# Lent weight room, one more kept K tile, a mean summed ahead and a new order in a two-layer decode kernel

## The chip, the core and the metric

The kernel runs on one core of a Trainium2 chip, as one launch. The metric is the device time of one execution in microseconds. Three runs of the kernel before gave 302.71, 304.16 and 307.49 us, median 304.16. One more execution was recorded by the profiler; all stretches and durations below come from it.

## What is computed

Four rows of 512 numbers (x) go through attention, a gated unit, the same attention and the same gated unit again; each step adds to x. Attention reads a cache of keys and values: 4 batch rows (b), 8 heads of keys and values, 4096 positions, 128 numbers each, bf16. Four query heads share one cache head. Both layers read the same cache and the same weights.

```python
def _A_ref(x, k_cache, v_cache, wq, wo):
    q = (x @ wq).reshape(B, Sq, Hq, Dh).transpose(0, 2, 1, 3)
    k = jnp.repeat(k_cache, rep, axis=1)
    v = jnp.repeat(v_cache, rep, axis=1)
    scores = jnp.einsum("bhqd,bhkd->bhqk", q, k) * (Dh ** -0.5)
    p = _softmax(scores, axis=-1)
    o = jnp.einsum("bhqk,bhkd->bhqd", p, v)
    return o.transpose(0, 2, 1, 3).reshape(B, Sq, Hq * Dh) @ wo
def _B_ref(x, w_gate, w_up, w_down):
    return (_sigmoid(x @ w_gate) * (x @ w_up)) @ w_down
x = A_x
x = x + _A_ref(_layernorm(x), k_cache, v_cache, wq, wo)
x = x + _B_ref(_layernorm(x), w_gate, w_up, w_down)
x = x + _A_ref(_layernorm(x), k_cache, v_cache, wq, wo)
x = x + _B_ref(_layernorm(x), w_gate, w_up, w_down)
```

## The kernel before

**Units.** Attention is cut into 16 units, each written b hg l: batch row b, head half hg (4 of the 8 cache heads), layer l. `UNITS` fixes their order: 000 010 100 011 110 200 001 111 210 300 211 310 101 201 311 301. A unit has 8 tiles of K and 8 of V: head s = 0 to 3, half of the positions q = 0 or 1, 512 KB each (128 partitions of 4096 bytes).

**Kept tiles.** Units with hg = 1 load their 16 tiles in layer 0 and leave them in place until layer 1 of the same row has used them (`tile` and `fresh`, lines 520 to 528: a tile is not loaded again where l = 1 and hg = 1). So 010 to 011, 110 to 111, 210 to 211 and 310 to 311 each hold 16 places. Units with hg = 0 load their tiles twice.

**The ring.** K and V tiles live in 23 places (`SLOTS`, the tensor `slots`). Weights have their own tensors: wq (two halves of 2 MB), wo (four parts of 1 MB), wg, wu and wd (1.75 MB each).

**The loads.** All loads are issued by SyncE (SP in the profile) in the order of the string `LOADS`, through `load_kv` (L544) and `load_w` (L552). A word is a weight or a piece of a unit: K2002 stands for two separate loads of unit 200, K010b for head 1 of unit 010 with both halves in one load of 1 MB, for which two neighbouring places must be free. SP works in order: if a load must wait for its place, all later loads wait behind it. The DMA engines work off what has been issued.

**A unit's work.** `queries` forms the unit's queries (PE, ACT) and writes them to `qz` (DVE, L739); for l = 1 it needs the finished x of its row. `unit_scores`: DVE transposes each freshly loaded K tile in place (L762), PE multiplies it with the queries into the PSUM bank `S_ps[i % 2]` (L770). `unit_probs`: the maximum, the exponential and a transposition (L792 to L837). `unit_values`: PE multiplies with the V tiles into `O_ps` (L900), ACT copies (L912), PE and DVE bring the result to `oT` (L919, L927); in layer 0 PE multiplies with wo and DVE adds to x (L941, L953). A place is free again when its last reader is done: PE L770 for K, PE L900 for V.

**The chain.** After unit b10, `chain(b)` runs the gated unit of row b in layer 0: `layer_norm` (L963 to L975; it uses `sq` as scratch), `rstd` (L984 to L993, the power on POOL), `gate_up` (L1003), `gated` (L1030 to L1042), `down` (L1055), x (L1078), and `layer_norm` and `rstd` again for the second attention. Units b01 and b11 cannot start their queries before it.

**The end.** The last V tiles to arrive are those of unit 301. `project` multiplies the last heads with wo (L1098, L1109). `last_chain` then forms the mean of x (DVE L1125, PE L1129 with a matrix of -1/512), subtracts it (`centre`, L1117), takes the squares (L1134, L1139, L1144, power L1151), runs the gated unit for all four rows at once (L1003, L1030, L1035, L1042), brings x into row form in three bf16 parts (L1175, copy L1179), multiplies with wd in 56 matmuls of 128 columns (L1185), joins both with one DVE instruction (L1194) and stores the output with four DMAs, two from SP and two from ACT (L1202).

**The planner.** All instructions are put into a plan with a cost, a rank and an optional shift per stage (`SHIFTS`); `_Plan.schedule` lists them per engine ahead of time: the instruction that can start first, and among equals the one of lowest rank. `slot_for` takes, for each load, the place that becomes free first. What it lists is the fixed order of each engine; waits are semaphores. Where PE would be idle it puts matmuls without use (L1228), which keep the clock up.

## Time and profile before

| | us |
|---|---|
| median of three runs | 304.16 |
| the profiled execution, its own time | 303.01 |
| its span, first to last instruction | 301.3 |
| PE busy | 221.0 |
| DVE busy, of it K transpositions (L762) | 168.2, 115.6 |
| ACT busy | 61.1 |
| granted TensorE clock, mean share | 0.977 |

The chain that ended last consists to 54% of the span of DMA transfers into `slots`, to 25% of PE and to 12% of DVE. 114.57 MB are loaded: 28 loads of 1 MB and 136 of 512 KB for K and V, and nine for the weights. In the parts of the page, a busy share is of one engine; DMA is the mean over the 16 DMA engines. A row of stretches gives, for a stretch of the span, its length, each engine's busy time with the count of instructions, the granted clock, the share of DMA and the rate in GB/s. In a row of the timeline stand the start, the duration, the engine, the line, the operation and, in brackets, the idle time of the engine ahead of it and what ended it.

### The profile page before, as it was taken

How to read it: one execution, taken by the hardware profiler on the slowest of the kernel's cores; microseconds unless marked ns; L12 is line 12 of the kernel's file. 1: busy time of each engine (PE TensorE's matmuls, PEld its weight loads, DVE VectorE, ACT ScalarE, POOL GpSimd, SP SyncE). 2: the span in 40 equal slices, each digit the busy share in tenths (PEclk: the TensorE clock that was granted, in tenths of full speed). 3: DMA queues.
4: the chain of work that ended last, by engine and by line, in shares of the span. 5: the costliest groups of instructions: out<-in, count | busy, mean ns of one | idle time of the engine just before them, and what ended most of it. 6: DMA issues, size and time to landing. Idle time of an engine off the chain costs nothing.

```text
span 301.3 us, 8952 instructions
## 1 busy us (share of the span) xinstructions
PE 221.0 (73%) x4010; PEld 134.8 (45%) x4010; DVE 168.2 (56%) x323; ACT 61.1 (20%) x154; POOL 13.0 (4%) x48
## 2 busy tenths in 40 slices
PE   1202504758797769887999798898986888989895
PEld 1201301435365436544566454446645445554463
DVE  4499436204214967795127977116899781287313
ACT  0200200200312210024322111422320233224211
POOL 8200000000000000000000000000000000000000
PEclk9999999998999997999999799999999799999999
DMA  6999999999999999999999999998899999999940
GB/s 256 429 422 413 419 390 424 407 401 412 415 421 381 328 401 411 411 414 407 407 407 406 411 413 413 411 397 333 289 405 413 406 411 408 410 399 406 406 172 3
DMA packets 28086, 115.14 MB, mean 382 GB/s; under 512 B 2832, under 2 KB 2832, under 8 KB 24336
## 3 DMA queue, kind: packets, MB, share of 16 engines
q1 hardware_dynamic: 28000, 114.57, 95.6%
q8 instruction: 31, 0.51, 0.7%
q14 instruction: 7, 0.06, 0.1%
q10 hardware_dynamic: 48, 0.01, 0.0%
HBM read 114.56 MB, written 0.00 MB: 380 GB/s over the span
## 4 chain that ended last, share of the span: by engine, by line
DMA 54%; PE 25%; DVE 12%; SPq 3%; issue 3%; ACT 2%; DVEq 0%; ACTq 0%
DMA slots<-in_A_v_cache_dram 29%; DMA slots<-in_A_k_cache_dram 25%; DVE slots L762 7%; PE O_ps L900 5%; PE S_ps L770 4%; PE PT_ps L1228 3%; SPq L544 3%; PE M_ps L941 2%; PE G_ps L1055 2%; PE M_ps L919 1%; PE Q_ps L690 1%; PE G_ps L1003 1%; PE Q_ps L706 1%; DVE stat L792 1%; SPq L552 1%
## 5 line engine op out<-in xcount | busy, mean ns | idle before, releaser
L762 DVE STREAM_TRANSPOSE slots<-slots 128x1024 int32<-128x1024 int32 x96 | 115.6, 1227 | 25.7 <-DMA slots<-in_A_k_cache_dram 24.3
L770 PE MATMUL S_ps<-slots,qz 128*32 128x512 bf16 x512 | 39.2, 431 | 36.5 <-DVE slots L762 34.7
L1228 PE MATMUL PT_ps<-even 128*128 128x256 bf16 x453 | 64.9, 283 | 1.2 <-ACT pt_sb L827 1.2
L1228 PEld LDWEIGHTS PT_ps<-even 128*128 128x128 bf16 x453 | 40.8, 101 | 18.9 <-issue 11.3
L900 PE MATMUL O_ps<-slots,pt_sb 128*16 128x512 bf16 x496 | 35.9, 383 | 16.0 <-DMA slots<-in_A_v_cache_dram 12.0
L770 PEld LDWEIGHTS S_ps<-slots,qz 128*32 128x32 bf16 x512 | 13.0, 101 | 52.9 <-DVE slots L762 38.2
L912 ACT ACTIVATE b<-O_ps 128x512 bf16<-128x512 f32 x31 | 18.5, 596 | 72.3 <-PE O_ps L900 59.4
L806 ACT ACTIVATE pp<-S_ps,tr 128x512 bf16<-128x512 f32 x16 | 13.3, 831 | 40.6 <-DVE tr L799 21.6
L900 PEld LDWEIGHTS O_ps<-slots,pt_sb 128*16 128x16 bf16 x496 | 9.1, 87 | 27.2 <-issue 14.1
L927 DVE TENSOR_TENSOR oT<-M_ps,rl 128x8 bf16<-128x8 f32 x31 | 4.7, 152 | 29.4 <-PE M_ps L919 29.1
L941 PE MATMUL M_ps<-oT,wo 128*128 128x64 bf16 x512 | 19.7, 195 | 0.9 <-DVE oT L927 0.6
L941 PEld LDWEIGHTS M_ps<-oT,wo 128*128 128x128 bf16 x512 | 17.5, 99 | 6.0 <-DVE oT L927 2.2
L792 DVE TENSOR_REDUCE stat<-S_ps 128x1 f32<-128x512 f32 x16 | 10.9, 681 | 9.4 <-PE S_ps L770 9.2
L919 PE MATMUL M_ps<-sel_o,b 128*64 128x64 bf16 x496 | 14.0, 200 | 2.4 <-ACT b L912 1.5
L919 PEld LDWEIGHTS M_ps<-sel_o,b 128*64 128x64 bf16 x496 | 10.6, 113 | 10.9 <-ACT b L912 6.2
L993 POOL TENSOR_TENSOR stat<-stat 128x1 f32<-128x1 f32 x8 | 4.4, 549 | 251.1 <-ACT stat L989 251.1
L827 ACT ACTIVATE pt_sb<-PT_ps 128x512 bf16<-128x512 f32 x16 | 9.5, 597 | 15.0 <-PE PT_ps L817 15.0
L953 DVE SCALAR_TENSOR_TENSOR x<-M_ps,x 128x4 f32<-128x4 f32 x16 | 2.4, 153 | 14.9 <-PE M_ps L941 14.9
L734 ACT ACTIVATE maskrs<-mask,stat 128x16 f32<-128x16 f32 x16 | 4.4, 301 | 23.3 <-DVE qz L739 22.0
L812 DVE STREAM_TRANSPOSE pp<-pp 128x256 int32<-128x256 int32 x16 | 6.9, 430 | 4.1 <-ACT pp L806 4.0
L1055 PE MATMUL G_ps<-pp,wd 128*128 128x64 bf16 x224 | 7.5, 191 | 2.1 <-issue 1.1
L739 DVE TENSOR_TENSOR qz<-Q_ps,maskrs 128x256 bf16<-128x256 f32 x16 | 6.3, 397 | 4.9 <-PE Q_ps L729 4.0
(133 smaller groups left out, 165.9 us busy)
## 6 DMA issues: line engine op xcount, KB each, us to landing
slots<-in_A_k_cache_dram SPq DMA_DIRECT2D x68, 512.0 KB, 8.2
slots<-in_A_v_cache_dram SPq DMA_DIRECT2D x68, 512.0 KB, 9.8
slots<-in_A_k_cache_dram SPq DMA_DIRECT2D x14, 1024.0 KB, 13.9
slots<-in_A_v_cache_dram SPq DMA_DIRECT2D x14, 1024.0 KB, 14.5
wq<-in_A_wq_dram SPq DMA_DIRECT2D x2, 2048.0 KB, 18.6
wo<-in_A_wo_dram SPq DMA_DIRECT2D x4, 1024.0 KB, 17.8
wg<-in_B_w_gate_dram SPq DMA_DIRECT2D x1, 1792.0 KB, 18.5
wu<-in_B_w_up_dram SPq DMA_DIRECT2D x1, 1792.0 KB, 17.3
```

Of the source, the lines that this page charges most:

```text
L544: return e.dma_start(o, src)
L762: "dve", lambda e, t=t: e.transpose(ring[t.slot].bitcast(dt.int32), ring[t.slot].bitcast(dt.int32)),
L770: fns.append(lambda e, s=s, t=t, nn=nn, q=q: e.matmul(S_ps[qi][32 * s:32 * s + 32, :], lhsT=window(qi, s * NQ + nn, q), rhs=ring[t.slot].r ...
L792: dve(lambda e: e.tensor_reduce(ml[at], bank, AX.X, ALU.max, negate=True), keys(f"S{qi}", ss), keys("ml", ss), 0.7)
L806: lambda e: e.activation(p_sb[at].rearrange("p (t j r) -> p t r j", j=32, r=2), bank.rearrange("p (t r j) -> p t r j", r=2, j=32), ACTF.Ex ...
L827: "act", lambda e: e.activation(pt_sb[qi][:, cols], PT_ps[:, cols], ACTF.Copy),
L900: fns.append(lambda e, m=m, at=at, v=v, c=c, q=q: e.matmul(O_ps[m:m + 16, :], lhsT=pt[:, at:at + 16], rhs=ring[v.slot][:, c * 512:(c + 1) ...
L912: "act", lambda e: e.activation(b1[:], O_ps[:], ACTF.Copy),
L919: fns.append(lambda e, tt=tt, r=r, a=a: e.matmul(M_ps[64 * a:64 * a + 64, r * SP:(r + 1) * SP], lhsT=b1[:, bass.ds(tt * P + r, 64, step=2) ...
L941: fns.append(lambda e, k=k, n=n, h0=h0: e.matmul(M_ps[:, k * MORE:(k + 1) * MORE], lhsT=wo[:, h0 + n, k * P:(k + 1) * P], rhs=oT[:, b, h0 ...
L1055: fns.append(lambda e, k=k, c=c, rows=rows: e.matmul(o_ps[:, k * MORE:(k + 1) * MORE], lhsT=wd[:, c, k * P:(k + 1) * P], rhs=rows.unsqueez ...
L1228: S.filler(lambda e: e.matmul(PT_ps[:, 0:256], lhsT=ident, rhs=flat_even[:, 0:256], start=True, stop=True), "PT")
```

## The change

- The string of the loads is another permutation of the same pieces, with one tile less: `EXTRA` names K tile (b 3, hg 0, s 3, q 1), which stays in the ring from unit 300 to unit 301 and is not loaded a second time. The loads of 1 MB are 40 instead of 28, and 512 KB loads 111 instead of 136. Which heads are loaded whole is now noted per unit and head.
- The planner's places are 23, then 2 for each part of wo, 3 each in wg, wu and wd, and 8 in wq. Places in wo, wg, wu and wd can be given to tiles until the weight's own load, which waits until they are no longer read (`lend`, `closes`). Places in wq can be used once the last instruction that reads that half of wq is done (`inherit`). A tile that is kept between layers (`stays`) is never put there. A 1 MB load needs two neighbours in the same tensor (`run`).
- The mean at the end: DVE sums the rows of wo for heads 8 to 15 (four reductions over 2 x 512 numbers, stage `sums`) and keeps the sums, times -1/512, as two bf16 parts. `mean_so_far` forms the mean of x before the last two projections; `mean_ahead` adds the share of the last eight heads, eight matmuls of four columns for each four heads, into the same PSUM bank. `last_chain` no longer has L1125 and L1129.
- The product with wd at the end has 28 matmuls of 256 columns; even and odd chunks go to separate halves of the partitions, except the last two. Two DVE instructions on 64 partitions x 256 join it (`lower`, then the output), x in row form is 64 x 256, and two DMAs store the output.
- `SHIFTS` has other values for most stages, so the order on every engine is another.

```diff
+EXTRA = "K3031"
-LOADS = "wq0 K100d K000b K000d K000a K010b K100c K000c K010d wq1 K010a V000a wo1 wo0 K1000 K010c V000c V000b V010b V010d wo2 V000d wo3 K1002 V010c wg V010a wu wd V100d V100c K0011 K2002 K2001 K2003 V1001 K2000 K0012 K110b K110a V1000 K1101 K1103 K0010 V110a K0013 V110b V1102 V1103 V2002 V2003 V2000 V2001 V0012 V0013 K3000 K2100 K3002 K3003 K210c K3001 K2102 K210d V0011 V2101 V0010 V2100 V210d V210c V3000 V3002 V3001 V3003 K2011 K3103 K2010 K1010 K3101 K1011 K1013 K3102 K3100 K1012 V3101 V3100 K2012 K2013 V3102 V3103 V1010 V1011 V2012 V2013 V1012 K3011 K3010 V1013 K3012 K3013 V2010 V2011 V3010 V3011 V301C V301D"
+LOADS = "wq0 K000a K000d K000c K000b wq1 K100c V000d wo0 V000a wg V000c wo2 K010d K1002 wo3 K010c K010a V000b K010b K1000 K100d V010a V010b wo1 V010d V010c wu wd V1000 V1001 K0013 K2002 K2003 K2000 K0011 V100c K2001 K110b K1101 K1103 K110a V100d K0010 V110a K0012 V110b V1102 V1103 V0010 V0011 V2002 V2003 V2000 V2001 K3000 K2100 K3001 V0013 K210c K210d V0012 K3003 K2102 V2101 K3002 V2100 V210d V210c V3002 V3000 V3003 V3001 K1012 K2011 K310b K1010 K310a K1011 K3101 K1013 K3103 K201a V310a K201b V310b K2013 V3102 V3103 V1010 V1011 V1012 V1013 K3013 V2012 K3011 V2013 K301b K301a V301b V201a V201b V301a V301C V301D"
...
+    def lend(self, slots, load):
+
+        load.closes = tuple(slots)
+        self.lent |= set(slots)
+
+    def inherit(self, slots, key):
+
+        t = _Tile(key)
+        t.users = [op for op in self.ops if key in op.keys]
+        for s in slots:
+            self.slots[s] = t
...
+            stays = any(t.stays for t in op.tiles)
+            for s, t in enumerate(tenants):
+                if s in closed or (stays and s in self.lent):
+                    until.append(None)
...
-                if None in until[s:s + n]:
+                if None in until[s:s + n] or self.run[s] != self.run[s + n - 1]:
...
+                    keepers = [u for s in op.closes if tenants[s] for u in tenants[s].users]
+                    if any(u.end is None for u in keepers):
+                        continue
+                    at = max([at] + [u.end + LATENCY[u.eng] for u in keepers])
...
+                for s in op.closes:
+                    if tenants[s]:
+                        op.deps |= set(tenants[s].users)
+                closed |= set(op.closes)
...
-    S = _Plan(SLOTS)
+    S = _Plan([SLOTS, 2, 2, 2, 2, 3, 3, 3, 8])
...
+    room(slots[:].rearrange("p a n -> p (a n)"), SLOTS)
+    for i in range(4):
+        room(wo[:, 8 * i:8 * i + 8].rearrange("p h n -> p (h n)"), 2, f"wo{i}")
+    for key, w in (("wg", wg), ("wu", wu), ("wd", wd)):
+        room(w[:].rearrange("p k n -> p (k n)"), 3, key)
+    room(wq[:].rearrange("p a k n -> p (a k n)"), 8, "wq")
+    double, ring = ring, [r[:, 0:TH * DH] for r in ring]
...
-    def fresh(kind, hg, l, s, q):
-        return not (l == 1 and hg == 1 and (s, q) in kept[kind])
+    def fresh(kind, b, hg, l, s, q):
+        return l == 0 or not (hg == 1 or (kind, b, hg, s, q) in extra)
...
-        S.put("sp", lambda e: e.dma_start(o, i), writes=[key], dma=key, size=size, cost=0.5)
+        op = S.put("sp", lambda e: e.dma_start(o, i), writes=[key], dma=key, size=size, cost=0.5)
+        S.lend(lent.get(key, ()), op)
...
+    mean_ps = S_ps[0][:, 0:B]
+
+    def mean_so_far(rank):
+
+        S.stage = "mean0"
         S.put(
             "dve", lambda e: e.tensor_reduce(xsum, x[:], AX.X, ALU.add),
             reads=[f"x{b}" for b in every_b], writes=[f"xsum{b}" for b in every_b], cost=0.2, rank=rank,
         )
         S.put(
-            "pe", lambda e: e.matmul(U_ps[:, 0:B], lhsT=ones, rhs=xsum, start=True, stop=True),
-            reads=["ones"] + [f"xsum{b}" for b in every_b], writes=["U"], cost=0.35, pairs=2, rank=rank,
-        )
+            "pe", lambda e: e.matmul(mean_ps, lhsT=ones, rhs=xsum, start=True, stop=False),
+            reads=["ones"] + [f"xsum{b}" for b in every_b], writes=keys("S0", range(NS)), cost=0.35, pairs=2, rank=rank,
+        )
+
+    def mean_ahead(h0s, rank):
+
+        S.stage = "mean1"
+        for h0 in h0s:
+            fns = []
+            for h in range(h0, h0 + 4):
+                for part in (0, 1):
+                    fns.append(lambda e, h=h, part=part, h0=h0: e.matmul(
+                        mean_ps, lhsT=wsum[:, part, h - 8:h - 7].broadcast_to([P, P]), rhs=oT[:, :, h],
+                        start=False, stop=(h0 == h0s[-1] and h == h0 + 3 and part == 1),
+                    ))
+            S.put(
+                "pe", fns, reads=[f"oT{b}{h0}" for b in every_b] + ["wsum"], writes=keys("S0", range(NS)), cost=0.0, rank=rank,
+            )
...
         for c0, c1 in cuts:
             fns = []
             for c in range(c0, c1):
                 h = pt_h[:, 64 * (c // 2):64 * (c // 2) + 64].rearrange("p (i r) -> p i r", r=2)[:, 0:B, c % 2]
-                for k in range(KD):
-                    fns.append(lambda e, k=k, c=c, h=h: e.matmul(
-                        S_ps[0][32 * k:32 * k + B, 0:P], lhsT=h, rhs=wd[:, c, k * P:(k + 1) * P], start=(c == 0), stop=(c == FB - 1),
+                upper = 64 * (c % 2) if c1 < FB else 0
+                for z in range(2):
+                    fns.append(lambda e, c=c, h=h, z=z, at=upper + 32 * z: e.matmul(
+                        S_ps[0][at:at + B, 0:256], lhsT=h, rhs=wd[:, c, z * 256:(z + 1) * 256], start=(c < 2),
+                        stop=(c == FB - 1 or (at >= 64 and c == cuts[-1][0] - 1)),
                     ))
...
         S.put(
             "dve",
             lambda e: e.scalar_tensor_tensor(
-                out=rows[:], in0=S_ps[0][:, 0:P], scalar=rs_row, in1=xrow, op0=ALU.mult, op1=ALU.add,
+                out=lower, in0=S_ps[0][64:, 0:256], scalar=rs_row[64:], in1=xrow, op0=ALU.mult, op1=ALU.add,
             ),
...
+        S.put(
+            "dve",
+            lambda e: e.scalar_tensor_tensor(
+                out=b1[0:64, 0:256], in0=S_ps[0][0:64, 0:256], scalar=rs_row[0:64], in1=lower, op0=ALU.mult, op1=ALU.add,
+            ),
+            reads=["S0h0", "rs_row"] + keys("pt_sb0", range(NS)), writes=[own("B1", True)], cost=0.4, rank=rank, lock="B1",
+        )
+        for z in range(2):
             S.put(
-                "act" if k % 2 == 0 else "sp",
-                lambda e, k=k: e.dma_start(out.rearrange("b s (k p) -> k (b s) p", p=P)[k], rows[32 * k:32 * k + B, :]),
-                reads=["xin"], writes=[f"out{k}"], dma="out", cost=0.1, rank=rank,
+                "act" if z == 0 else "sp",
+                lambda e, z=z: e.dma_start(out.rearrange("b s (z p) -> z (b s) p", z=2)[z], b1[32 * z:32 * z + B, 0:256]),
+                reads=[own("B1")], writes=[f"out{z}"], dma="out", cost=0.1, rank=rank,
             )
...
+    S.stage = "sums"
+    for n in range(0, 8, 2):
+        S.put(
+            "dve", lambda e, n=n: e.tensor_reduce(row_sums[:, n:n + 2], wo[:, 8 + n:10 + n, :], AX.X, ALU.add),
+            reads=["wo1"] + ["sq"] * (n > 0), writes=["sq"] if n == 0 else [f"sums{n}"], cost=1.1, rank=rank_v((3, 0, 1), 0),
+        )
+    S.put(
+        "act", lambda e: e.activation(wsum[:, 0], row_sums, ACTF.Copy, scale=-1.0 / D),
+        reads=["sq", "sums2", "sums4", "sums6"], writes=["wsum"], cost=0.2, rank=rank_v((3, 0, 1), 0),
+    )
+    S.put(
+        "dve",
+        lambda e: e.scalar_tensor_tensor(out=wsum[:, 1], in0=row_sums, scalar=-1.0 / D, in1=wsum[:, 0], op0=ALU.mult, op1=ALU.subtract),
+        reads=["sq"], writes=["wsum"], cost=0.17, rank=rank_v((3, 0, 1), 0),
+    )
...
+    mean_so_far(rank_v((3, 0, 1), 0) + 1.0)
     project(8, range(4), rank_v((3, 0, 1), 1) + 1.0, "U")
+    mean_ahead(sorted((8, 12), key=lambda h: place["v", (3, 0, 1), h // 4, 1]), rank_v((3, 0, 1), 1) + 0.5)
     project(8, range(4, 8), rank_v((3, 0, 1), 1) + 1.0, "G")
     last_chain(rank_v((3, 0, 1), 1) + 2.0)
...
+    for i in range(2):
+        S.inherit(lent["wq"][4 * i:4 * i + 4], f"wq{i}")
```

More of the change, by code (lines that the diff above doesn't have):

```diff
@@ L78, in __init__ @@
         self.readers = {}
[L79 removed]
+        self.run = [r for r, n in enumerate(runs) for _ in range(n)]
+        self.slots = [None] * len(self.run)
+        self.lent = set()
         self.stage = ""
```

90 lines of the change are left out of this document (49 added, 41 removed).

## The prediction

> **What bounds the kernel now.** I read the page's slices first, then a table of stretches, then the waits and the timeline of SP, then the timeline of the end.
>
> ```profile
> DMA  6999999999999999999999999998899999999940
> GB/s 256 429 422 413 419 390 424 407 401 412 415 421 381 328 401 411 411 414 407 407 407 406 411 413 413 411 397 333 289 405 413 406 411 408 410 399 406 406 172 3
> HBM read 114.56 MB, written 0.00 MB: 380 GB/s over the span
> ```
>
> The DMA engines are busy nearly all the time; no other engine is above 73%. The rate sags twice, at slices 13 and 14 and at 28 and 29, and there is a tail without transfers. Stretches put numbers to it (last two columns: DMA share, GB/s):
>
> ```profile
> 4.00:94.00 90.00, 44.88 (x748) 28.31 (x748) 39.51 (x67) 10.69 (x25) 5.47 (x25) 0.98 1.02 414
> 94.00:108.00 14.00, 11.62 (x224) 6.65 (x225) 11.94 (x18) 4.26 (x13) 0.55 (x1) 1.00 0.97 341
> 108.00:200.00 92.00, 79.03 (x1362) 48.86 (x1360) 54.56 (x104) 19.96 (x46) 1.10 (x2) 0.96 1.02 411
> 200.00:220.00 20.00, 18.23 (x395) 11.88 (x394) 13.02 (x24) 6.21 (x20) 1.10 (x2) 1.00 0.89 330
> 220.00:286.00 66.00, 55.71 (x1018) 31.89 (x1010) 42.81 (x81) 17.17 (x41) 1.10 (x2) 0.97 1.03 408
> ```
>
> Against 411 GB/s the first sag costs (411 - 341) / 411 x 14 = 2.4 us, the second 81 / 411 x 20 = 3.9 us. Outside them the stream is full. Why the sags come is seen at SP:
>
> ```profile
> SPq L544 <- PE O_ps L900: 77.3, 18, 15.9
> ...
> 95.16 1.83 SPq L544 DMA_DIRECT2D slots<-in_A_k_cache_dram  x2
> ...
> 199.46 0.33 SPq L544 DMA_DIRECT2D slots<-in_A_v_cache_dram  x1
> 199.83 4.31 SPq L544 DMA_DIRECT2D slots<-in_A_k_cache_dram  x3
> ```
>
> SP waits for a place until PE has read a V tile, once for 15.9 us. At 95.16 SP has issued 38.5 MB (counted along `LOADS`), and by the rates above some 38 MB have landed: nothing is queued. The second stop ends at 199.46, when the queue is again short. Both times 16 places hold a kept unit (010, then 210) and seven rotate. They come free when 011 and 211 have run, that is after chain(0) and chain(2): 211's queries are ready at 211.59 (L739) and its scores run 212.07 to 214.09 (L770).
>
> The end:
>
> ```profile
> 292.42 0.64 PE L1098 MATMUL G_ps<-oT,wo 128*128 128x64 bf16 x16
> 293.17 0.17 DVE L1109 TENSOR_TENSOR x<-G_ps,x 128x16 f32<-128x16 f32 x1 [0.80 <-PE G_ps L1098]
> ...
> 293.60 0.39 PE L1129 MATMUL U_ps<-stat 128*128 128x4 f32 x2
> ...
> 294.03 0.17 DVE L1117 TENSOR_TENSOR maskrs<-x,U_ps 128x16 f32<-128x16 f32 x1 [0.48 <-PE U_ps L1129]
> ...
> 298.71 0.35 DVE L1194 SCALAR_TENSOR_TENSOR rows<-S_ps,stat,pt_sb 128x128 bf16<-128x128 f32 x1 [0.70 <-issue]
> 299.09 0.66 SPq L1202 DMA_DIRECT2D out_dram<-rows  x2
> 299.10 0.80 ACTq L1202 DMA_DIRECT2D out_dram<-rows  x2
> ```
>
> From the last V matmul (291.16) to the end of the span lie 10.1 us, one step behind the other.
>
> **The change, part by part.** The sum goes against the profiled 303.01 us (span 301.3 and 1.7 around it); the median is 1.15 higher, two of the three runs lie within 1.2 of it.
>
> *One K tile less:* 0.524 MB / 411 GB/s = 1.28 us, since the stream is the bound. Its transposition goes too (L762, 1.23 us), off the path.
>
> *Twelve more loads of 1 MB in place of 24 halves, 12.58 MB:* the stretch 12 to 20 us, all whole loads, ran at 422 GB/s, 140 to 160, all halves, at 407. That makes 30.9 - 29.8 = 1.1 us at most; the stretch 108 to 200, which mixes them, shows 411, so the bound below is 0. I take 0.6, about the middle. The Trainium skill, "DMA: Bandwidth & Descriptors", section "Rules for kernel authors", asks for at least 1 MiB per DMA for full bandwidth; by that page's 435 GB/s ceiling the term would be an estimated 2.0 us, and the measured 422 says less.
>
> *Room in wo, wg, wu and wd:* nothing gained by itself. It exists only until wd is issued (68.4 before), and 4 to 94 us already runs at 414. Both orders have the same 40 tiles and all weights ahead of V100, 34.9 MB, so wd lands and chain(0) goes on at the same time (before, ACT waits for wd until 89.60). The new wait stands at SP, with every later load behind it. Its cover is the queue: wd was issued 21 us before its use.
>
> *Room in wq:* free only after the queries of 311 and 301 (the last near 271). 220 to 286 runs at 408, so it gains nothing; it pays back the kept tile's place at the end.
>
> *First sag, 2.4 us:* behind wd came V100d and V100c, heads 3 and 2 whole, so the first values could start only when both had landed, and places came free at 95.1. Now V1000 comes first, half 0 of heads 0 and 1: usable 1.05 MB, 2.5 us, sooner, and two places return then. Seven places of K still fill up before 011's scores (98.65), so part stays. Bounds 0 and 2.4; I take 1.2.
>
> *Second sag, 3.9 us:* the count. V210c ends at 76.8 MB, near 192.5 us; K210's places return near 214 and bring data 2 us later: 24 us x 0.411 = 9.7 MB, 18.4 tiles, should go out meanwhile. V300's eight are used and released; some 10.4 K tiles are stuck, with seven places: 3.4 tiles x 1.28 = 4.4 us, near the 3.9 seen. The kept tile, loaded at 70.5 MB, takes one of the seven: +1.28. Against that, chain(2) has slack: the power L993 ran at 210.66 because L984 stood behind the query matmuls, V300's second half was there near 203 but read at 206.0 behind L1055 (1.84 us). With those better placed 211 comes 0.4 to 2 us sooner; bounds of the whole term -2.0 and +2.6 (two tiles), I take +0.3.
>
> *Sums:* four DVE reductions of 1024 numbers, 1.2 us each by L762's 1.23 for as many elements, 5 us with the two small ones. wo1 lands near 73 us; from 75 to 94 DVE works about 5 us. Nothing, by that idle time; without it up to 1.2 us ahead of one transposition, or ahead of chain(0), whose ACT square needs `sq`.
>
> *The end.* L1125 and L1129 with their gaps fill 293.34 to 294.03: -0.69. The last eight matmuls of `mean_ahead` stand ahead of L1098 or just behind it: 16 of L1098 take 0.52 to load, so eight about 0.26: net -0.43. The wd product streams as many columns per strip as before, with half the instructions: 0. The second of the two joining DVE instructions has 256 columns instead of 128; L1035 with 192 took 0.33, with 448 0.62, so 0.41 against 0.35, and `lower` may still run when the last matmuls end: +0.1. One output DMA per queue instead of two: ACT issued for 0.80, so -0.4. Together -0.73; bounds -1.1 and -0.2.
>
> Sum: 303.01 - 1.28 - 0.6 - 1.2 + 0.3 - 0.73 = **299.5 us**.
>
> **The rivals.**
>
> *A, the forecast:* 299.5, own range 297.0 to 301.5. Chance 0.40.
>
> *B, both sags mostly go:* the new order of the chain steps frees 211's places and V300's sooner. 303.0 - 1.3 - 1.1 - 0.7 - 2.4 - 2.0 = 295.5 (294.5 to 298.0). For it: the late reads at 206 and 210.66. Against: the count, by which a shift of 2 us returns at most 1.6 tiles while one place is gone. Chance 0.37.
>
> *C, the kept tile costs a place and no order helps:* second sag +1.28, first unchanged, whole loads 0: 303.0 - 1.28 - 0.7 + 1.28 = 302.3. Chance 0.07.
>
> *D, slower, pairs that aren't free:* K310b and K310a, 1 MB each, stand fourth to sixth in the order behind V300, in the second sag, and need two neighbouring places; unit 310 is kept, so weight rooms are closed to them. Before, all loads there were halves. If no pair is free until 211 has released K210 (214), SP stands from the fourth tile on: three more tiles are late, 3.8 us, plus 1.28 for the place, and with a shorter queue the stretch behind it runs like 200 to 220. 303.0 - 2.6 + 3.8 + 1.3 = 305.5, and more where K201 and V310, also whole, repeat it. It decides if the pair comes later than 203.3, when K2011's second tile went out. Chance 0.13, of it 0.06 above 310.
>
> *E, a weight dams the queue:* a weight's load waits for tiles in its room. From rows: the queue covers about 6.8 MB / 0.411 = 16 us behind wd's issue at 68.4; if the last K100 tile there is read after 84, each microsecond costs one, and chain(0) with it. Before, K1002 was transposed from 71.31. Five too late: 304.5. In the Trainium skill, same page, the section on the anatomy of one DMA has it that DMA engines never wait on semaphores; the issuing sequencer does. The 15.9 us stop of SP agrees. Chance 0.03, of it 0.01 above 310.
>
> **How the numbers follow.** About 2% is what a measurement of this kernel can tell from no change: 298.1 and 310.2 around the median. Faster: B's 0.37 and 0.06 of A, 0.43. Slower: 0.07 from D and E. Within: 0.50. The range 294.6 to 304.8 takes in A, C, E and nearly all of B, and leaves out most of D.
>
> **What would show it.** Bytes 114.04 MB. The stretch 94 to 108 above 341 GB/s, near 375. A sag between 195 and 220 that is still there, about 4 us; if it is gone, B; if SP stops ahead of K310b, D. The first 90 us at 414 or a little more. From the last V matmul to the end of the span 9.4 us instead of 10.1, with no reduction and no matrix of -1/512 between L1098's successor and the centring. I am wrong if the DMA stream is no longer what ends last before the tail.

## The result and the profile after

The changed kernel takes 302.26 us, the median of 20 runs (300.39 to 304.69), against 304.01 us of 20 runs of the kernel before beside it: ratio 0.9937, 95% interval 0.9916 to 0.9959. It is 0.6% faster, which is no change by the bound of 2%. The forecast of 299.5 us lies 4.5 us below the 304.01; 1.75 came. A ratio and its interval leave out runs more than 1.5% above the fastest of their kernel, so that it can differ from the quotient of the medians, which are over all runs.

The profiled execution of the changed kernel took 303.67 us (span 301.9), 1.4 above its own median; that of the kernel before was 1.0 below its. So the two profiles are compared stretch by stretch, and a reading counts where other runs with the same order repeat it. In the changed kernel's lines the loads of K and V are L590 (before L544), transpositions L811, scores L819, V matmuls L949, queries L739 (before L690), `qz` L788, the last projection L1147. The page of the changed kernel, DMA busy tenths and rate by slices, and the bytes:

```profile
DMA  7999999999999999999999999999799999999920
GB/s 255 426 412 407 413 408 405 422 421 407 412 413 408 405 417 415 415 412 403 399 396 361 395 414 416 406 345 358 277 404 418 417 409 388 395 385 416 417 94 1
HBM read 114.04 MB, written 0.00 MB: 378 GB/s over the span
```

The first sag (slices 13 and 14) is gone. There is a new one at slice 22 (361), the one at 27 to 29 is deeper (345, 358, 277), and 34 to 36 are below 400. The same five stretches as before, DMA share and GB/s last:

```profile
4.00:94.00 90.00, 47.46 (x759) 29.94 (x760) 43.00 (x72) 11.11 (x26) 5.46 (x25) 0.81 1.02 413
94.00:108.00 14.00, 12.32 (x240) 7.87 (x241) 12.36 (x17) 4.16 (x13) 0.55 (x1) 1.00 1.03 409
108.00:200.00 92.00, 78.32 (x1343) 47.38 (x1345) 54.63 (x105) 20.32 (x49) 1.10 (x2) 0.94 1.02 402
200.00:220.00 20.00, 17.87 (x365) 11.22 (x365) 12.60 (x24) 6.22 (x18) 1.10 (x2) 0.91 0.85 320
220.00:286.00 66.00, 54.29 (x1024) 31.62 (x1020) 41.44 (x77) 16.69 (x41) 1.10 (x2) 1.00 1.01 406
```

A finer cut, each rate also as time lost against 411 GB/s, (411 - rate) / 411 x length; the last column is the range over three variants with the same loads and another end (below):

| stretch | before | after | the three variants |
|---|---|---|---|
| 94 to 108 | 341, 2.4 us | 409, 0.1 us | 396 to 402 |
| 140 to 170 | 408, 0.2 us | 389, 1.6 us | 383 to 387 |
| 195 to 220 | 345, 4.0 us | 331, 4.9 us | 332 to 341 |
| 245 to 270 | 408, 0.2 us | 394, 1.0 us | 394 to 400 |

So 2.3 us of the first sag are won, and 1.4 + 0.9 + 0.8 us are lost in three later stretches. (They are readings of one profiled execution; the last column shows how far they repeat.) The largest new loss leads to PE, in the second chain. Changed kernel, timeline of PE (start, duration, line, count, idle time before):

```profile
155.62 0.97 PE L739 MATMUL Q_ps<-small,wq 128*128 128x32 bf16 x32
156.43 0.36 PE L1033 MATMUL U_ps<-stat 128*128 128x1 f32 x2
156.66 0.55 PE L739 MATMUL Q_ps<-small,wq 128*128 128x32 bf16 x16
157.14 0.61 PE L949 MATMUL O_ps<-slots,pt_sb 128*16 128x512 bf16 x8
157.68 0.32 PE L739 MATMUL Q_ps<-small,wq 128*128 128x32 bf16 x6
159.07 0.40 PE L739 MATMUL Q_ps<-small,wq 128*128 128x32 bf16 x10 [1.08 <-issue]
...
160.96 3.56 PE L819 MATMUL S_ps<-slots,qz 128*32 128x512 bf16 x32 [0.24 <-DVE qz L788]
```

The same place in the kernel before:

```profile
156.62 0.96 PE L690 MATMUL Q_ps<-small,wq 128*128 128x32 bf16 x32
157.43 0.36 PE L984 MATMUL U_ps<-stat 128*128 128x1 f32 x2
157.66 0.95 PE L690 MATMUL Q_ps<-small,wq 128*128 128x32 bf16 x32
158.54 0.39 PE L900 MATMUL O_ps<-slots,pt_sb 128*16 128x512 bf16 x2
159.36 0.60 PE L900 MATMUL O_ps<-slots,pt_sb 128*16 128x512 bf16 x6 [0.44 <-issue]
...
160.84 1.99 PE L770 MATMUL S_ps<-slots,qz 128*32 128x512 bf16 x32
```

The chain came 1.0 us earlier (x of row 1 at 154.48 instead of 155.48), yet 111's scores began 0.1 us later and took 3.56 instead of 1.99 us. PE stopped for 1.08 us with 10 of the 64 query matmuls left ("issue": nothing that the profile shows was waited for); in the kernel before a stop of 0.44 us fell amid V matmuls, behind the queries. While the scores ran, the granted clock was low: from 160 to 165 it was 1.00 before, and in the changed kernel 0.66 (the column ahead of the last two):

```profile
160.00:165.00 5.00, 4.76 (x69) 2.04 (x64) 3.21 (x5) 0.31 (x1) 0.00 (x0) 0.66 0.98 377
```

The places of K110 come free with those scores, so SP stood: the second half of V0013 went out at 162.85 and K210c at 164.55; before, SP had K210c out at 162.31.

The end, from oT on:

```profile
292.64 0.16 DVE L922 TENSOR_TENSOR oT<-M_ps,rl 128x4 bf16<-128x4 f32 x1
292.77 0.36 PE L1174 MATMUL S_ps<-stat 128*128 128x4 f32 x2
292.99 0.56 PE L1185 MATMUL S_ps<-oT,wsum 128*128 128x4 bf16 x16
...
293.42 0.63 PE L1147 MATMUL G_ps<-oT,wo 128*128 128x64 bf16 x16
...
297.65 0.50 PE L1258 MATMUL S_ps<-wd,pp 128*4 128x256 bf16 x12
...
...
298.40 0.71 PE L1258 MATMUL S_ps<-wd,pp 128*4 128x256 bf16 x16
299.02 0.49 DVE L1268 SCALAR_TENSOR_TENSOR pt_sb<-S_ps,stat,pt_sb 64x256 f32<-64x256 f32 x1 [0.75 <-issue]
299.55 0.47 DVE L1275 SCALAR_TENSOR_TENSOR b<-S_ps,stat,pt_sb 64x256 bf16<-64x256 f32 x1
300.05 0.34 SPq L1283 DMA_DIRECT2D out_dram<-b  x1
```

From the last V matmuls (291.47) to the end of the span are 10.44 us, against 10.10 before. The last projection (293.42) comes 0.78 us behind oT, before 0.22 (292.20 to 292.42), since 16 of the new matmuls and the matrix of the mean stand ahead of it; and the second join waits for the first, 0.49 + 0.47 us where one took 0.35. The first join, `lower`, was to run beside the last matmuls; it began at 299.02, and the row of the last matmuls ends at 299.11.

### The profile page after: what moved, and what is told of

The parts are those of the page before. It is cut to its first block, busy times and chain, and to the rows that moved or that the text cites. A ratio compares the mean times of both kernels' runs of the same rounds, so it can differ in the third digit from the quotient of the medians.

```text
span 301.9 us, 8919 instructions
## 1 busy us (share of the span) xinstructions
PE 222.5 (74%) x3996; PEld 136.0 (45%) x3996; DVE 171.4 (57%) x328; ACT 61.7 (20%) x155; POOL 13.0 (4%) x48
## 3 DMA queue, kind: packets, MB, share of 16 engines
q1 hardware_dynamic: 26120, 114.04, 94.7%
HBM read 114.04 MB, written 0.00 MB: 378 GB/s over the span
## 4 chain that ended last, share of the span: by engine, by line
DMA 35%; PE 34%; SPq 15%; DVE 7%; issue 4%; ACT 3%; POOL 0%; DVEq 0%; ACTq 0%
DMA slots<-in_A_v_cache_dram 18%; SPq L590 14%; DMA slots<-in_A_k_cache_dram 11%; PE S_ps L819 7%; DMA wo<-in_A_v_cache_dram 6%; PE O_ps L949 6%; PE PT_ps L1326 4%; PE M_ps L990 3%; PE G_ps L1104 2%; PE Q_ps L739 2%; DVE slots L811 2%; PE M_ps L968 2%; PE G_ps L1052 2%; SPq L598 1%; PE Q_ps L755 1%
## 5 line engine op out<-in xcount | busy, mean ns | idle before, releaser
L811 DVE STREAM_TRANSPOSE slots<-slots 128x1024 int32<-128x1024 int32 x90 | 108.2, 1226 | 29.7 <-DMA slots<-in_A_k_cache_dram 28.7
L1326 PE MATMUL PT_ps<-even 128*128 128x256 bf16 x451 | 63.8, 285 | 6.5 <-DVE slots L811 6.5
L819 PE MATMUL S_ps<-slots,qz 128*32 128x512 bf16 x492 | 39.2, 437 | 20.2 <-DVE slots L811 17.6
L1326 PEld LDWEIGHTS PT_ps<-even 128*128 128x128 bf16 x451 | 41.7, 102 | 23.2 <-issue 10.4
L949 PE MATMUL O_ps<-slots,pt_sb 128*16 128x512 bf16 x468 | 37.6, 401 | 18.6 <-DMA slots<-in_A_v_cache_dram 10.8
L819 PEld LDWEIGHTS S_ps<-slots,qz 128*32 128x32 bf16 x492 | 13.0, 102 | 37.6 <-DVE slots L811 20.2
L949 PEld LDWEIGHTS O_ps<-slots,pt_sb 128*16 128x16 bf16 x468 | 9.7, 90 | 29.7 <-issue 19.3
L968 PE MATMUL M_ps<-sel_o,b 128*64 128x64 bf16 x496 | 14.4, 203 | 4.2 <-ACT b L961 2.2
L788 DVE TENSOR_TENSOR qz<-Q_ps,maskrs 128x256 bf16<-128x256 f32 x16 | 6.4, 401 | 6.5 <-PE Q_ps L778 4.3
L739 PE MATMUL Q_ps<-small,wq 128*128 128x32 bf16 x256 | 8.0, 177 | 1.9 <-issue 1.9
L739 PEld LDWEIGHTS Q_ps<-small,wq 128*128 128x128 bf16 x256 | 7.3, 97 | 3.8 <-issue 2.5
L1084 DVE SCALAR_TENSOR_TENSOR b<-pp,U_ps 128x448 bf16<-128x448 f32 (+2 forms) x7 | 3.3, 480 | 10.2 <-ACT pp L1079 9.7
```

The lines of the kernel that those rows point to most:

```text
L739: fns.append(lambda e, c=c, k=k: e.matmul(Q_ps[:, c * WIDE:(c + 1) * WIDE], lhsT=wq[:, hg, k, c * DH:(c + 1) * DH], rhs=xT[:, b, k:k + 1]. ...
L811: "dve", lambda e, t=t: e.transpose(ring[t.slot].bitcast(dt.int32), ring[t.slot].bitcast(dt.int32)),
L819: fns.append(lambda e, s=s, t=t, nn=nn, q=q: e.matmul(S_ps[qi][32 * s:32 * s + 32, :], lhsT=window(qi, s * NQ + nn, q), rhs=ring[t.slot].r ...
L949: fns.append(lambda e, m=m, at=at, v=v, c=c, q=q: e.matmul(O_ps[m:m + 16, :], lhsT=pt[:, at:at + 16], rhs=ring[v.slot][:, c * 512:(c + 1) ...
L968: fns.append(lambda e, tt=tt, r=r, a=a: e.matmul(M_ps[64 * a:64 * a + 64, r * SP:(r + 1) * SP], lhsT=b1[:, bass.ds(tt * P + r, 64, step=2) ...
L1326: S.filler(lambda e: e.matmul(PT_ps[:, 0:256], lhsT=ident, rhs=flat_even[:, 0:256], start=True, stop=True), "PT")
```

## The experiments

Medians of one group of runs share the kernel before, named with each. A single run has no interval.

**The end taken apart.** Three variants of the changed kernel: `a_oldend` (mean and wd product as before), `a_oldmean` (mean as before and no row sums, new product) and `a_oldprod` (new mean, old product). The edits put the kernel before's lines back; with the product come back x in row form, the one join and the four output DMAs. In the code `...` stands for lines left out. The mean as before, in `a_oldend` and `a_oldmean`:

```diff
-    mean_so_far(rank_v((3, 0, 1), 0) + 1.0)
...
+            "pe", lambda e: e.matmul(U_ps[:, 0:B], lhsT=ones, rhs=xsum, start=True, stop=True),
```

The product as before, in `a_oldend` and `a_oldprod`:

```diff
-                for z in range(2):
...
+                for k in range(KD):
+                    fns.append(lambda e, k=k, c=c, h=h: e.matmul(
+                        S_ps[0][32 * k:32 * k + B, 0:P], lhsT=h, rhs=wd[:, c, k * P:(k + 1) * P], start=(c == 0), stop=(c == FB - 1),
...
```

> The kernel after with the end of the kernel before (mean formed at the end, 56 matmuls of 128 columns, one joining instruction, four output DMAs; no row sums of wo); loads, places and the order up to the last V tiles are the plan's of after. Read: from the first of the last 16 matmuls on V to the end of the span (before 10.10 us, after 10.44). Theory 1, the new end itself is the loss (two joining instructions one behind the other, the mean's matmuls ahead of the last projection): 10.0 to 10.1. Rival, the late unit 301 in the new order is the loss, and the new end gained what was forecast: 10.8 or more. The stretch 140 to 170 us, if its dip of after (383 and 368 GB/s per 10 us at 150 and 160) belongs to the order: again below 390; if to that one execution: 404 to 407 as before.

> The kernel after with the mean formed at the end as before (reduction and matrix of -1/512 behind the last projection; no row sums of wo), the new product with wd and its joins kept. Last V matmul to the end of the span: if the mean ahead saves the 0.43 us forecast, 10.9; if its 16 small matmuls and the first mean stand ahead of the last projection and give it all back, 10.4 to 10.5.

> The kernel after with the product with wd, its joining instruction and the four output DMAs of before, the mean ahead kept. Last V matmul to the end of the span: if the two joins in series cost more than the two DMAs saved, 10.1 to 10.3; if the new product and the two DMAs saved 0.3 us as forecast, 10.7.

One run each: 302.16, 302.64 and 303.11 us (before 305.05). From the last V matmuls, as the expectations count, the tails are 10.24, 10.56 and 10.07 us: 10.24 and 10.56 fall between the two cases expected, nearer to a new end that loses and to a mean known ahead that gives its gain back; 10.07 is the case in which the joins cost more than the DMAs save. 140 to 170 ran at 383 in `a_oldend`, so that dip belongs to the order. The whole times differ by what the stream does before the end (last byte at 289.71, 289.90 and 290.87 us), and oT comes 1.17 us behind the last V matmuls in all three and in the changed kernel, 1.05 before; so the end is read from oT to the end of the span: before 9.06, `a_oldend` 9.07, `a_oldmean` 9.39, `a_oldprod` 8.90, changed kernel 9.27. The mean known ahead saves 0.17 (9.07 to 8.90) and 0.12 (9.39 to 9.27); the new product with its joins and DMAs costs 0.32 and 0.37. In `a_oldprod` the product begins at 297.51 and the output is issued at 299.21, 1.70 later, with 2.18 to the end; in the changed kernel 297.65 to 300.05 are 2.40, and 1.86 are left. The DMAs bring 0.32 of the 0.4 forecast. The other 0.70 is lost in the joins: from the first matmul to the first join are 1.33 us in `a_oldprod` and 1.37 in the changed kernel, from there to the issue 0.37 and 1.03.

**Room in the weights, one kind at a time.** `a_wqonly` lends wq alone, `a_nowq` all but wq:

```diff
-    S = _Plan([SLOTS, 2, 2, 2, 2, 3, 3, 3, 8])
+    S = _Plan([SLOTS, 8])                        # a_wqonly
...
-    for i in range(4):
-        room(wo[:, 8 * i:8 * i + 8].rearrange("p h n -> p (h n)"), 2, f"wo{i}")
...
+    S = _Plan([SLOTS, 2, 2, 2, 2, 3, 3, 3])      # a_nowq
...
-        S.inherit(lent["wq"][4 * i:4 * i + 4], f"wq{i}")
```

> The kernel after, its places those of the ring and of wq alone; the room in wo, wg, wu and wd isn't lent. Forecast's view, the early room buys nothing by itself: 4 to 94 us at 413 GB/s within 4, 94 to 108 at 400 or more as in after. Rival, the early room is what closed the first sag: 94 to 108 falls towards 341. In the second sag the kept tiles then lie in other places: if the 1 MB loads of unit 310 must wait for two neighbours, 200 to 220 falls from 320 to 290 or less and the time rises by 2 to 3.5 us over after, to about 305; if neighbours don't matter it stays at 320 and about 302.3.

Measured: 304.55 us (before 305.05), ratio 0.9992 (0.9952 to 1.0032), where the changed kernel has 0.9937 (0.9916 to 0.9959). 94 to 108 ran at 404: up to there the early room is worth nothing, as forecast. But 195 to 220 fell to 289 (in a profile 3 us above its own median), since K310b, a load of 1 MB, found no pair of neighbouring places until 211 had given back K210: SP issued it at 213.54, in the changed kernel at 206.28. The waits of SP between 195 and 220, first of `a_wqonly`, then of the changed kernel (195 to 216; total, times, longest):

```profile
SPq L586 <- PE O_ps L945: 12.8, 3, 7.8
SPq L586 <- PE S_ps L815: 6.7, 1, 6.7
```

```profile
SPq L590 <- PE O_ps L949: 10.5, 2, 7.4
SPq L590 <- PE S_ps L819: 5.4, 1, 5.4
```

Here the wait of 6.7 stands ahead of K310b, in the changed kernel that of 5.4 one load later, with 1 MB more on its way. In this variant, then, where the early tiles lie decided about a pair some 130 us later.

> The changed kernel without the room in wq, the rest as it is. The forecast put that room at nothing, since 220 to 286 ran at 408 before. Theory (with one place taken by the kept tile and pairs to be found, it pays at the end): 245 to 270 at 350 to 375 GB/s instead of 394, time 303.5 to 304.8. Rival (the forecast): 245 to 270 at 390 or more, time 302.0 to 302.6.

Measured: 305.54 us in one run (before 304.71), 0.7 above the theory's range, and

```profile
245.00:270.00 25.00, 21.71 (x476) 13.29 (x469) 10.29 (x27) 8.11 (x23) 1.10 (x2) 1.00 0.96 369
270.00:286.00 16.00, 13.13 (x252) 7.79 (x248) 9.38 (x21) 4.21 (x9) 0.00 (x0) 1.00 0.96 392
```

against 394 and 413 in the changed kernel: 25/411 x 25 + 21/411 x 16 = 2.3 us. The room in wq holds this stretch up; the size rests on one execution of each.

**The first sag by the order of V100 alone.** In the kernel before, V1000 V1001 change places with V100d V100c in `LOADS`.

```diff
-LOADS = "... wu wd V100d V100c K0011 K2002 K2001 K2003 V1001 K2000 K0012 K110b K110a V1000 K1101 ..."
+LOADS = "... wu wd V1000 V1001 K0011 K2002 K2001 K2003 V100d K2000 K0012 K110b K110a V100c K1101 ..."
```

> The kernel before, with V1000 V1001 (half 0 of two heads each) loaded first of unit 100's values and V100d V100c (whole heads) later, in each other's places. Only 94 to 108 us is read; what follows was planned for the other order. Theory (the forecast's: the first sag is the wait for both whole heads, so the order of these loads alone closes it): 94 to 108 at 385 to 410 GB/s instead of 341. Rival (it takes the rest of the order, chain(0)'s new place among it): 335 to 365.

Measured: 94 to 108 at 343, so the rival holds (time 307.02, not comparable). Timeline of PE in that run:

```profile
91.73 0.39 PE L900 MATMUL O_ps<-slots,pt_sb 128*16 128x512 bf16 x4 [1.90 <-DMA slots<-in_A_v_cache_dram]
92.06 3.17 PE L1055 MATMUL G_ps<-pp,wd 128*128 128x64 bf16 x56
95.16 0.54 PE L900 MATMUL O_ps<-slots,pt_sb 128*16 128x512 bf16 x4
```

Half 0 of two heads was read at 91.73, but PE's order had the next four V matmuls, which finish these two places, behind all 56 of the wd product; SP went on at 95.74 (before 95.16). In the changed kernel eight V matmuls stand between two halves of the product and SP went on at 92.65:

```profile
91.07 1.00 PE L1104 MATMUL G_ps<-pp,wd 128*128 128x64 bf16 x28 [1.20 <-issue]
92.00 0.61 PE L949 MATMUL O_ps<-slots,pt_sb 128*16 128x512 bf16 x8
92.54 1.01 PE L1104 MATMUL G_ps<-pp,wd 128*128 128x64 bf16 x28
```

So the order of the loads alone does not close the sag. The changed kernel has both that order and V matmuls amid the product; PE's order alone was not run.

**The stop on PE.** Matmuls are counted from the program's start, a product in f32 (x2 in the rows) once. The stops over 0.4 us between a wd product and the scores behind it stand in both kernels behind the same matmuls: the 841st (amid 011's queries, changed kernel), the 1716th (both), the 2466th (in both 10 matmuls ahead of the end of 211's queries; in the kernel before the count is off by two). These lie 7 x 125 and 6 x 125 apart. In the kernel before:

```profile
207.40 1.52 PE L690 MATMUL Q_ps<-small,wq 128*128 128x32 bf16 x54
209.75 0.41 PE L690 MATMUL Q_ps<-small,wq 128*128 128x32 bf16 x10 [0.84 <-issue]
```

The 1716th has a stop in nine of the runs here, at 158.4 to 160.0 us: both kernels, the three variants of the end, `a_wqonly`, `a_nowq`, `b_v100first` and `c_newtail40`. `a_wide70` shifts the count: where two fillers stand side by side, one of twice the width takes their place.

```diff
+            if op in fillers and order and order[-1] in fillers and len(order[-1].fns[0:1]) and order[-1].fns[0] is self.fill and op.start > 98.0 and merged < 70:
+                order[-1].fns = [self.wide]
+                order[-1].deps |= op.deps
+                merged += 1
+                continue
...
+             lambda e: e.matmul(PT_ps[:, 0:512], lhsT=ident, rhs=flat_even[:, 0:512], start=True, stop=True), "PT")
```

> The changed kernel with 70 pairs of neighbouring filler matmuls of 256 columns between 98 and about 170 us made into single ones of 512 columns: the same columns, 70 instructions fewer on PE ahead of and around the second chain; nothing else moves. In the traces so far PE stops for 0.4 to 1.3 us behind the same matmul counted from the program's start, the 1716th (in the kernel before amid V matmuls, in the changed one 10 matmuls ahead of the end of 111's queries) and behind the 2466th, whatever stands there. Theory (the stop is tied to the count, and it is what holds back 111 and with it the loads of 150 to 170): no stop over 0.4 us between L1104's line and the first scores in the second and the third chain; 111's scores begin about 1 us earlier against the x update of the same chain (6.5 us behind it in the changed kernel, 5.5 here), clock of 160 to 165 near 1.0 instead of 0.66 to 0.83; 140 to 170 at 398 to 408 GB/s instead of 382 to 389; 195 to 220 at 340 or more; time 299.8 to 301.3. Rival 1 (places and load order set the stretch 140 to 170, the stop only fills a wait): stop gone, but 140 to 170 under 392 and time 301.8 to 302.6. Rival 2 (the stop belongs to the wait of a semaphore, not to the count): it stays ahead of the last 10 matmuls of the queries.

Measured: 300.56 us in four runs (before 304.71), ratio 0.99 (0.9824 to 0.9976). No stop over 0.4 us is left in the second and third chain. Timeline of PE, then the stretches:

```profile
156.31 0.55 PE L748 MATMUL Q_ps<-small,wq 128*128 128x32 bf16 x16
156.79 0.61 PE L958 MATMUL O_ps<-slots,pt_sb 128*16 128x512 bf16 x8
157.33 0.57 PE L748 MATMUL Q_ps<-small,wq 128*128 128x32 bf16 x16
...
159.57 2.08 PE L828 MATMUL S_ps<-slots,qz 128*32 128x512 bf16 x32 [0.43 <-DVE qz L797]
```

```profile
160.00:165.00 5.00, 4.63 (x73) 2.67 (x66) 4.90 (x10) 1.07 (x3) 0.00 (x0) 1.00 1.03 403
...
140.00:170.00 30.00, 26.36 (x548) 15.92 (x546) 13.71 (x32) 9.10 (x25) 1.10 (x2) 1.00 1.02 408
195.00:220.00 25.00, 21.89 (x471) 14.15 (x471) 15.36 (x29) 7.07 (x22) 1.10 (x2) 1.00 0.90 348
```

The order around the queries is the same, V matmuls and all; 111's scores now begin 5.44 us behind the x update (154.13) instead of 6.48, at full clock, and 140 to 170 is back at 408. The theory holds in each number, and both rivals fall: the stop is tied to the count, and it took the larger part of the first sag's gain away. The other runs say the same. In the seven in which the stop stands among 111's queries (the changed kernel, the three variants of the end, `a_wqonly`, `a_nowq`, `c_newtail40`), 140 to 170 runs at 374 to 389 and the clock of 160 to 165 is 0.66 to 0.83; in the four of the changed kernel's kind without it (`a_wide70`, `a_one_less_kept`, `c_hand40`, `d_less_wide`), 400 to 408 and 1.00. The time itself is less sure: 1.7 us below the changed kernel by the medians, 1.1 by the ratios, and the intervals overlap.

The same edit in the kernel before:

> The kernel before with 70 pairs of fillers between 98 and about 170 us made single ones of 512 columns, nothing else. In the kernel before the stop behind the 1716th matmul hit no query, that behind the 2466th stood 10 matmuls ahead of the end of 211's (0.84 us). Theory (the stops act through the queries alone): the second goes, 195 to 220 rises from 345 to 350 to 360 GB/s, 140 to 170 stays near 408, time 303.0 to 303.7, so that the change with the stops out of both is worth 2.4 to 3.1 us instead of 1.75. Rival (the wider fillers help in another way, the clock for one): as much as in the changed kernel, 302.4 or less.

Measured: 303.55 us (before 304.68), ratio 0.9972 (0.9937 to 1.0006); 140 to 170 at 404, 195 to 220 at 370, above the range expected. No stop is left ahead of 211's scores. The rival is out. With the stops out of both, the change is worth 300.56 against 303.55, 3.0 us by the medians of two groups of runs, 2.2 by the ratios. The second sag is then 1.3 us deeper than before: 348 against 370 over 25 us.

**The kept tile.** `a_one_less_kept` keeps the 16 tiles of 310 as before and loads the other one twice, with `SHIFTS` and `LOADS` found anew for it.

```diff
-EXTRA = "K3031"
+EXTRA = ""
```

> The changed kernel without the additional kept K tile (0.52 MB more to load, one place more for loading between the layers), its orders of loads and work found anew for that count. The first term of the forecast says +1.28 us for the tile, the second sag says -1.28 for the place. Theory (the two cancel, keeping it is worth nothing here): bytes 114.56 MB, 195 to 220 about 10 to 20 GB/s above the changed kernel's 331, time within 0.6 us of 302.3. Rival (the tile is a gain of its own, the place isn't short): 195 to 220 at 325 to 340 as in the changed kernel and the time 303.0 to 304.0.

Measured: 303.91 us (before 304.71), ratio 0.9996 (0.995 to 1.0042), so the rival's time; but 195 to 220 fell to 311, as neither said, since a stop of 1.25 us stood ahead of the last 25 of 211's queries. So once more, with the wide fillers:

> The kernel without the additional kept tile (0.52 MB more to load), with 70 pairs of its fillers made single ones of 512 columns as in the run before of the changed kernel with wide fillers, so that the stop behind the 2466th matmul, which stood 25 matmuls ahead of the end of 211's queries (1.25 us), falls amid 211's scores. Only the kept tile (and the order that goes with it) then differs from that run (300.56 us, 195 to 220 at 348 GB/s). Theory (the tile is worth its bytes, 1.28 us, and the place costs less than that): no stop over 0.4 us ahead of 211's scores, 195 to 220 at 340 to 360, time 301.5 to 302.3. Rival (tile and place cancel): 195 to 220 at 360 to 375, time 300.2 to 301.0.

Measured: 302.39 us (before 304.46), ratio 0.9915 (0.9881 to 0.995), 0.1 above the theory's range; no stop ahead of 211's scores, and

```profile
195.00:220.00 25.00, 21.49 (x451) 13.55 (x451) 14.46 (x29) 6.70 (x21) 1.10 (x2) 1.00 0.91 344
```

which is near the 348 of `a_wide70`. The tile costs no place that shows in this stretch, and the rival is out. The time is above `a_wide70`'s by 1.8 us by the medians and by 0.5 by the ratios, whose intervals overlap, so the 1.28 us of its bytes are neither confirmed nor refuted; and the order of loads and work is another. (The profiled run has one more stop, of 1.66 us at 266.)

**A better end.** `c_newtail40` puts the eight matmuls of `mean_ahead` that read the last oT behind the last projection; `c_hand40` adds the old product and wide fillers, 40 of them already before 90 us.

```diff
-                "pe", fns, reads=[f"oT{b}{h0}" for b in every_b] + ["wsum"], writes=keys("S0", range(NS)), cost=0.0, rank=rank,
+                "pe", fns, reads=[f"oT{b}{h0}" for b in every_b] + ["wsum"], writes=keys("S0", range(NS)), cost=0.0, rank=rank + 40.0 * (h0 == h0s[-1]),
```

> The changed kernel, and of the matmuls of the mean known ahead the eight that read the last oT stand behind the last projection. Only the tail is read. Theory (the eight, and the matrix behind the late reduction, held the projection up): projection about 0.2 us behind oT, tail 9.8 to 10.0 us instead of 10.44. Rival (the centring then waits for the eight): tail 10.3 or more.

> The changed kernel with three edits: pairs of fillers made into single ones of 512 columns, 40 of them before 90 us and 30 behind 98 us (so that the stop behind the 841st matmul, 0.4 to 0.5 us amid 011's queries, falls behind 011's scores as well); the wd product, the joins and the four output DMAs of the kernel before; and of the matmuls of the mean known ahead, the eight that read the last oT behind the last projection instead of ahead of it. Theory: no stop over 0.4 us between wd product and scores in any of the three chains; 94 to 108 at 402 or more, 140 to 170 near 408; the last projection about 0.2 us behind oT instead of 0.78, and the tail (last 16 V matmuls to the end of the span) 9.4 to 9.7 us, against 10.07 with the old product alone and 10.44 in the changed kernel; time 299.2 to 300.0. Rival: the matrix of the mean then comes last instead of the projection, the tail stays at 10.0 and the time near 300.2.

`c_newtail40`: 302.68 us in one run (before 304.68). The tail is 10.25, between the two expectations, and the projection came 0.57 us behind oT instead of 0.2; from oT the end takes 9.08 instead of 9.27. `c_hand40`: 300.87 us (before 304.68), ratio 0.9855 (0.9798 to 0.9912), the lowest ratio of all, with an interval that reaches past the 2%, but slower than theory and rival had it (299.2 to 300.2); no such stop in any of the three chains, but a tail of 10.1 as the rival said, since oT came late behind the V matmuls (1.40 us, with two projections between). From oT it is 8.71, against 8.90 with the old product alone. Its timeline shows why the gain is 0.2 and not 0.5:

```profile
290.27 0.16 DVE L933 TENSOR_TENSOR oT<-M_ps,rl 128x4 bf16<-128x4 f32 x1
290.41 0.36 PE L1185 MATMUL S_ps<-stat 128*128 128x4 f32 x2
290.63 0.35 PE L1196 MATMUL S_ps<-oT,wsum 128*128 128x4 bf16 x8
...
290.84 0.63 PE L1158 MATMUL G_ps<-oT,wo 128*128 128x64 bf16 x16
```

The matrix of the mean still stands ahead of the projection, 0.57 us behind oT: x of the heads before it is ready too late for it.

## Why the prediction was right and wrong

The time lies in the range, and the side (a little faster, within 2%) was the likeliest, but the size was not: 1.75 us instead of 4.5. Of these 4.5, the terms of the sum make 3.5; the other 1.0 was in no term, since the sum started from a profiled execution 1.0 below the median. Rival C's 302.3 meets the measured 302.26 by luck: the first sag did not stay, and no row shows the price that it puts on the kept tile.

*The step that failed:* the sum took a sag that closes as won. Nothing in it asked whether the next wall of the same ring (the next unit whose places must come free before loading goes on) would come earlier as well. The stream reached unit 111's wall earlier, and 111's places did not come earlier: a stop of 1.08 us and a clock of 0.66 kept them back, and 1.4 us were lost in a third sag (140 to 170) that no term had. `a_wide70`, without the stops of the second and third chain, has 140 to 170 back at 408. The stop was visible before (0.84 us at 209.75, "issue", among the query matmuls); the forecast noted the queries' end at 211.59 and did not ask what held them.

*The end, -0.73:* wrong in sign, +0.34 from the last V matmuls, of it 0.21 from oT on. The mean known ahead gives 0.12 to 0.17 instead of 0.43, as 16 of its matmuls and the matrix stand ahead of the projection, 0.56 us where 0.26 was reckoned for eight. The joins, put at +0.1 because `lower` was to run beside the last matmuls, cost 0.66: there was no such overlap. The product cost 0.04; the DMAs, -0.4, gave 0.32.

*Room in wq, 0:* wrong, about 2.3 us. "220 to 286 runs at 408" described a kernel without the additional tile and without pairs; with them the stretch needs the room, and still runs at 394 from 245 to 270.

*Room in wo, wg, wu, wd, 0:* right up to 108 us, wrong behind it. Without it K310b found no pair until 213.54, which is rival D's mechanism. In the changed kernel D did not come: K310b went out at 206.28, later than the 203.3 that D names, but 0.48 us behind the load ahead of it, so that SP did not stand for it. By the ratios the early room is worth some 1.7 us (2.3 by the medians), with intervals that just overlap.

*First sag, -1.2:* 2.3 us, but the mechanism was half of it. The new order of the loads alone left the stretch at 343 (`b_v100first`); in the changed kernel V matmuls also stand amid the wd product, which the forecast had not seen. That the term came out larger than forecast is no merit of its reasoning.

*Second sag, +0.3:* 0.9 by the profile, 0.2 to 0.8 in the three variants. The count behind it agreed with the 3.9 us seen by chance: V210c landed near 195.0 (issued at 180.62, 14.4 us to landing), and 192.5 is V210d's landing. From 195.0 on the same count leaves 1.4 tiles, 1.8 us.

*Whole loads, -0.6:* about right, 0.5. The twelve additional ones all lie behind 206 us (K310, K201, V310, K301, V201, V301), and where most of them land the stream is a little faster: 220 to 245 at 414 instead of 410, 270 to 286 at 413 instead of 405. In the three profiles with the loads of the kernel before, or nearly so, these are 410 to 411 and 404 to 405; in the variants of the end 414 and 413 to 416, but in `a_wide70` the second is 406, and no run has the twelve as halves. The Trainium skill's rule of 1 MiB per DMA ("DMA: Bandwidth & Descriptors", "Rules for kernel authors") has the right direction in these rows, but with that page's 435 GB/s the estimate was 2.0 us.

*One K tile less, -1.28:* the bytes are 114.04 MB, as forecast, and the tile's place has no price that shows; the time is not resolved (above). *Sums, 0:* no loss shows; they took 1.16 to 1.21 us each, between 75.1 and 80.7.

Together, forecast against rows: end 0.9, third sag 1.4, 245 to 270 0.8, second sag 0.6, whole loads 0.1, less 1.1 of the first sag: 2.7 us of the 3.5 that the terms sum to. That would leave 0.8, where the medians say 1.75 and the two profiled executions lie 0.7 the other way. The rows place the losses; they do not add up to the medians.

## What to carry to other kernels

Where a ring of places feeds a stream, a stall that goes away pays only as far as the next wall moves too: list every wall, with what releases it and when, before a term is booked as won. An edit that changes the number of instructions moves an engine's stops; look where "issue" gaps stand in the chain that releases the walls. Matmuls put ahead "to be known early" cost at the end whatever stands behind them.

## What the hardware showed unexpectedly

PE's stops go with its code. The trace has the queue that the page calls "instruction": 31 packets, 0.51 MB, each 16,384 bytes. In the changed kernel one runs from 156.50 to 157.60 and PE goes on at 159.07; others end at 96.45 and 207.25, and PE goes on at 97.95 and 208.71; in the kernel before 158.07 and 159.36, 208.48 and 209.75. So PE resumes 1.3 to 1.5 us after a packet has landed, each time behind a multiple of 125 matmuls from the last such stop; with as many weight loads that is 250 instructions. The page's row:

```profile
q8 instruction: 31, 0.51, 0.7%
```

The 31 packets also fit the whole program: 3944 matmuls and as many weight loads are 254 instructions for each. And over all 14 profiles, all 32 stops of PE over 0.35 us that are marked "issue" and lie outside the wd products end 1.2 to 1.6 us behind the landing of a packet. (The stop of 1.20 us at 91.07, ahead of a wd product, is another thing: it ends 0.1 us behind DVE's transposition of `pp`, 90.39 to 90.97, and 3.5 us behind a packet.) That the packet is what PE waits for is inferred from these times and from the shift in `a_wide70`; no run changed the queue itself. Why a packet starts when it does (156.50 here, some 3 us after the count had passed the 1591st matmul) stays open.

A stop of 1.08 us with little other work (PE busy 2.92 of 4 us from 156 to 160) was followed by a clock of 0.66 over the next 5 us, 0.67 to 0.83 in the six other runs with that stop among 111's queries, and 1.00 in the kernel before and in `a_wide70`. A stop of 0.85 us at 159.99 in `b_v100first` did not lower it (1.00), so what decides is open.
